# A two-block attention kernel: a hardware loop with another start and end, wq loads at other places, and a wait moved behind a branch

## The chip, the cores and the metric

The kernel runs on one core of one Trainium2 chip. The metric is the device time of one execution in microseconds (us); all times given are medians of several runs. A profile's span leaves out about 1.7 us of what is timed (777.2 against 778.9 us for the profiled run of the kernel before).

Engine names in the profile: PE is TensorE (matmul), PEld its weight loads, DVE VectorE, ACT ScalarE, POOL GpSimd, SP SyncE, which issues all loads here. A "q" behind a name (SPq) means the sequencer of that engine.

## The reference

Two independent attention blocks A and B, with the results side by side. Each has 16 batches of 64 queries, 32 heads of 128 and 512 cached keys, in bfloat16.

```python
def _A_ref(x, k_cache, v_cache, wq, wo):          # B is the same on its own data
    B, Sq, D = x.shape                            # 16, 64, 640
    H, Dh = 32, 128
    q = (x @ wq).reshape(B, Sq, H, Dh).transpose(0, 2, 1, 3)
    scores = jnp.einsum("bhqd,bhkd->bhqk", q, k_cache) * (Dh ** -0.5)
    p = softmax(scores, axis=-1)
    o = jnp.einsum("bhqk,bhkd->bhqd", p, v_cache)
    return o.transpose(0, 2, 1, 3).reshape(B, Sq, H * Dh) @ wo
return jnp.concatenate([a, b], axis=-1)
```

The caches alone are 4 x 67 MB, read once.

## The kernel before

The work is cut into 128 packs. A pack is two batches by four heads: 2 MB of K and V in four loads of 512 KB. Four packs share one x tile; 32 packs make a phase (half of the heads of one block), and each phase needs four wq and four wo blocks of 640 KB.

A plan is made in Python: each operation gets a wished time in units of packs (the table AT), each engine's program is its operations in that order, and the semaphore waits are derived. TensorE's operations are XT (transpose of x), QP (q projection), S (scores), TR (transpose of the normalised weights, two a pack), PV and OP (output projection). They are staggered, so that QP of pack n stands beside PV and OP of pack n-2.

```python
class Cfg:
    NK = 6; NV = 4; NXN = 1; NWS = 4 ...          # buffers: packs of K, of V; x tiles; wq blocks
    PERIOD = 4
    FIRST = 4
    ...
# loads: (wished time, earliest time, rank, op); SyncE issues them in this order, one after the other
for ph in range(NPH):
    for j in range(NJ):
        w = ph * NJ + j
        n0 = ph * PH + j                          # PH = 32 packs a phase
        twp = n0 + (AT["WP1"] if ph else AT["WP0"])   # when wq is copied into its place
        ...
        ready = ...                               # when the staging buffer is free again
        loads.append((twp - 0.3, ready, 1, op))
...
# TensorE's program has a period of four packs: the middle becomes a hardware loop
pe = progs["pe"]
lo = next(i for i, o in enumerate(pe) if o.kind == "QP" and o.idx == cfg.FIRST)
hi = next(i for i, o in enumerate(pe) if o.kind == "QP" and o.idx == cfg.FIRST + cfg.PERIOD)
size = hi - lo
reps = (N - 1 - cfg.FIRST) // cfg.PERIOD
...
for op in prog[:lo]:
    emit(e, op, p, {})
with e.Fori(0, reps):
    for i, op in enumerate(prog[lo:lo + size]):
        emit(e, op, p, taken)                     # ... and takes back what semaphores counted in a turn
for op in prog[lo + size * reps:]:
    emit(e, op, p, taken)
```

Softmax is computed without subtracting a maximum. A flag tells at the end whether all sums stayed in range; if not (never with these inputs), a general program runs. The end of every engine's program:

```python
def run(e, eng):
    run_program(e, eng, 0)
    if eng == "act":
        all_done(e, 0, ("d_out",))                # all stores have landed
    e.wait_ge(sems[0][("s_flc",)], 1)             # the flag is known
    with e.register("flag_" + eng) as r:
        e.reg_load(r, flag[0:1, 0:1])
        with e.If_ne(r, 128):
            all_done(e, 0)
            run_program(e, eng, 1)                # the general program, skipped by a branch
            if eng == "act":
                all_done(e, 1, ("d_out",))
```

## Time and profile before

| What | Value | Where it is read |
|---|---|---|
| time | 778.7 us | median of the runs |
| DMA rate, 20 to 738 us | 378 to 401 GB/s | the page's slices |
| TensorE's own pace | 5.4 us a pack | start to start of QP, 90 to 165 us |
| one K or V load | about 1.31 us of the DMA's time | spacing of the landings |
| one wq or wo load | about 1.7 us | the same |
| last V of the last pack lands | 755.4 us | landings |
| PV of the last pack starts | 767.1 us | timeline |
| last store issued, end of the span | 771.15, 777.2 us | timeline |

The page's slices: 40 equal stretches of the span, 19.4 us each, with PE's and the DMA's busy tenths and what the DMA moved in GB/s.

```profile
PE   3868999998978999998977999999977899999974
...
DMA  9999999999999999999999999999999999999960
GB/s 313 388 395 397 396 393 397 393 396 393 389 388 399 399 398 401 399 394 398 387 387 393 397 397 397 396 398 398 386 378 389 395 398 400 399 400 399 400 258 16
```

DMA never falls below 9 until the last two slices, while PE dips to 7 at three places. Those are the phase boundaries: up to eight weight blocks are loaded there between K and V, and TensorE waits. The page's chain that ended last, by engine, does not say so clearly:

```profile
PE 41%; SPq 25%; DMA 18%; POOL 5%; issue 5%; DVE 4%; ACT 0%; DVEq 0%; ACTq 0%
```

PE has 41% of it because the chain is followed back from the end, and late in the run PE and the DMA have nearly the same pace: a V lands 0.25 to 0.7 us before its PV.

The tail is different. PE's timeline around the loop's end (start us, busy us, engine, line, operation, tiles, shapes, count; in brackets the idle time before it and what ended it):

```profile
738.35 0.38 PE L672 MATMUL ps<-wo_sb,oT_ring 128*128 128x512 bf16 x1
740.60 0.23 PE L675 MATMUL ps<-wo_sb,oT_ring 128*128 128x128 bf16 x1 [1.87 <-issue]
...
743.38 1.09 PE L593 MATMUL ps<-kt_ring,qs_ring 32*64 32x512 bf16 x25
747.01 0.65 PE L593 MATMUL ps<-kt_ring,qs_ring 32*64 32x512 bf16 x7 [2.54 <-issue]
...
748.54 0.31 PE L675 MATMUL ps<-wo_sb,oT_ring 128*128 128x128 bf16 x1 [0.34 <-issue]
```

PE stops twice, for 1.87 and 2.54 us, and the profile shows nothing that it waited for ("issue"). The loop was left at 733.6 us, so this is straight code that runs for the first time. The trace has 16 KB packets on the queue "q8 instruction" that start at 738.0 and 744.6 us, beside each stop. After the second, matmuls take longer (0.31 us for the output projection's narrow one instead of 0.23): the granted clock is 0.5 for 3.4 us from 746.9. The same reading as sums, PE's waits from 730 to 750 us (what waited, for what: us in total, times, longest):

```profile
PE ps L593 <- issue: 2.5, 1, 2.5
PE ps L675 <- issue: 2.5, 4, 1.9
PE ps L570 <- issue: 0.3, 1, 0.3
```

Three windows of 30 to 33 us (busy us of each engine, count of instructions, granted PE clock, DMA share, GB/s); the third is a phase boundary, the other two are not:

```profile
240.00:270.00 30.00, 28.04 (x860) 20.34 (x858) 23.14 (x38) 19.57 (x54) 16.11 (x25) 1.00 1.04 399
430.00:460.00 30.00, 28.27 (x851) 20.20 (x833) 23.60 (x40) 20.93 (x57) 15.40 (x23) 1.00 1.04 397
550.00:583.00 33.00, 26.86 (x822) 19.45 (x813) 21.67 (x38) 18.89 (x52) 21.86 (x28) 1.00 1.04 379
```

SyncE's own waits are short (the rest of its time it issues: its 560 issues take 712.4 us together, one from 0.33 to 5.02 us), against 12.5 us that a load needs from issue to landing. That is the DMA's time for about nine loads of 1.31 us; in this sense the data queue is called full below, and empty, or nearly so, when the DMA's rate has fallen off at the end (59 GB/s from 750 to 760 us):

```profile
SPq L535 <- PE ps L656: 15.6, 17, 4.9
SPq L528 <- PE ps L593: 9.5, 7, 2.6
...
SPq L509 <- PE ps L549: 4.9, 3, 2.6
```

The end of ScalarE's program, from the trace's records (start us, duration in ns):

```
DMA_DIRECT2D    771.15   338    the last store
EVENT_SEMAPHORE 771.52    17    waits for the flag
TENSOR_LOAD     773.47   478    reads the flag; held back until the store has landed
COMPARE_BRANCH  773.97    54    branches over the general program
DRAIN           776.89    80    the end
```

### The profile page before, as it was taken

The numbers are of one execution on the slowest core, as the hardware profiler recorded it, in microseconds if no ns is written. First come the engines' busy times: TensorE is split into PE (matmuls) and PEld (weight loads), VectorE is DVE, ScalarE is ACT, GpSimd is POOL, SyncE is SP. The second block draws the span as 40 slices with busy tenths as digits, with TensorE's granted clock in tenths as the row PEclk, the third lists the DMA queues.
The fourth block names the chain that finished last, engine by engine and source line by source line (L and its number), as shares of the span: only waits on it lengthen the run. The fifth ranks groups of instructions, "written<-read, shape, count | busy, mean of one in ns | idle before, by whom it ended". The sixth has DMA issues, their size and how long they took to land.

```text
span 777.2 us, 44414 instructions
## 1 busy us (share of the span) xinstructions
PE 674.1 (87%) x20001; PEld 492.0 (63%) x20129; DVE 544.4 (70%) x934; ACT 484.3 (62%) x1297; POOL 404.8 (52%) x582
## 2 busy tenths in 40 slices
PE   3868999998978999998977999999977899999974
PEld 2546677676756676666654676677655567677653
DVE  3546778787767777776755777777755678787753
ACT  2546767776655667665655676777655566666642
POOL 5524455555944454544863545454575355554532
PEclk9999999999999999999999999999999999999999
DMA  9999999999999999999999999999999999999960
GB/s 313 388 395 397 396 393 397 393 396 393 389 388 399 399 398 401 399 394 398 387 387 393 397 397 397 396 398 398 386 378 389 395 398 400 399 400 399 400 258 16
DMA packets 130099, 295.24 MB, mean 380 GB/s; under 512 B 9216, under 2 KB 31744, under 8 KB 130048
## 3 DMA queue, kind: packets, MB, share of 16 engines
q1 hardware_dynamic: 127744, 292.06, 99.4%
q10 hardware_dynamic: 2304, 2.62, 0.9%
q8 instruction: 17, 0.28, 0.2%
q14 instruction: 34, 0.28, 0.1%
HBM read 292.03 MB, written 2.62 MB: 379 GB/s over the span
## 4 chain that ended last, share of the span: by engine, by line
PE 41%; SPq 25%; DMA 18%; POOL 5%; issue 5%; DVE 4%; ACT 0%; DVEq 0%; ACTq 0%
SPq L528 12%; SPq L535 11%; PE ps L570 9%; PE ps L656 9%; PE ps L593 8%; DMA v_ring<-in_B_v_cache_dram 7%; PE ps L672 6%; POOL pn_ring L628 5%; PE ps L637 5%; DMA v_ring<-in_A_v_cache_dram 5%; PE ps L675 4%; DMA wo_sb<-in_B_wo_dram 2%; DMA kn_ring<-in_B_k_cache_dram 2%; DMA wo_sb<-in_A_wo_dram 2%; DVE pT_ring L644 2%
## 5 line engine op out<-in xcount | busy, mean ns | idle before, releaser
L628 POOL TENSOR_SCALAR pn_ring<-p_ring,recip 128x512 bf16<-128x512 bf16 x512 | 344.4, 692 | 344.0 <-DVE recip L623 343.7
L608 ACT ACTIVATE p_ring<-ps 128x512 bf16<-128x512 f32 x512 | 300.6, 593 | 163.4 <-PE ps L637 160.2
L583 DVE STREAM_TRANSPOSE kt_ring<-kn_ring 128x1024 f32<-128x1024 f32 x256 | 312.8, 1229 | 79.9 <-DMA kn_ring<-in_B_k_cache_dram 47.7
L644 DVE COPY pT_ring<-ps 128x1024 bf16<-128x1024 bf16 x256 | 176.2, 688 | 78.8 <-PE ps L637 72.6
L570 PE MATMUL ps<-xT_ring,wqp_sb 128*128 128x128 bf16 x2560 | 170.6, 223 | 19.8 <-issue 13.6
L570 PEld LDWEIGHTS ps<-xT_ring,wqp_sb 128*128 128x128 bf16 x2560 | 151.0, 115 | 28.8 <-issue 16.4
L656 PE MATMUL ps<-pT_ring,v_ring 64*128 64x64 bf16 x8192 | 142.7, 191 | 24.2 <-DMA v_ring<-in_B_v_cache_dram 11.1
L593 PE MATMUL ps<-kt_ring,qs_ring 32*64 32x512 bf16 x4096 | 148.0, 398 | 8.5 <-issue 6.1
L656 PEld LDWEIGHTS ps<-pT_ring,v_ring 64*128 64x128 bf16 x8192 | 127.3, 95 | 38.9 <-DMA v_ring<-in_B_v_cache_dram 14.5
L637 PEld LDWEIGHTS ps<-ident,pn_ring 64*128 64x128 bf16 x4096 | 74.6, 95 | 108.6 <-ACT oT_ring L663 58.9
L663 ACT ACTIVATE oT_ring<-ps 128x512 bf16<-128x512 f32 x128 | 76.4, 597 | 95.0 <-PE ps L656 73.5
L675 PE MATMUL ps<-wo_sb,oT_ring 128*128 128x128 bf16 x512 | 112.8, 220 | 23.2 <-issue 18.1
L637 PE MATMUL ps<-ident,pn_ring 64*128 64x64 bf16 x4096 | 105.1, 192 | 17.2 <-DVE pT_ring L644 11.2
L672 PE MATMUL ps<-wo_sb,oT_ring 128*128 128x512 bf16 x384 | 119.4, 382 | 0.0
L608 ACT ACTIVATION_READ_ACCUMULATOR p_ring<-ps 128x1 f32 x512 | 101.7, 199 | 0.0
L576 ACT ACTIVATE qs_ring<-ps 128x512 bf16<-128x512 f32 x128 | 76.4, 597 | 23.4 <-PE ps L570 23.4
L672 PEld LDWEIGHTS ps<-wo_sb,oT_ring 128*128 128x128 bf16 x512 | 50.1, 98 | 53.3 <-issue 1.1
L593 PEld LDWEIGHTS ps<-kt_ring,qs_ring 32*64 32x64 bf16 x4096 | 56.0, 104 | 42.7 <-issue 8.0
L685 DVE TENSOR_TENSOR acc<-acc,ps 128x128 f32<-128x128 f32 x96 | 27.4, 285 | 37.4 <-PE ps L675 37.2
L675 PEld LDWEIGHTS ps<-wo_sb,oT_ring 128*128 128x128 bf16 x512 | 50.5, 99 | 2.2 <-issue 2.2
L623 DVE RECIPROCAL recip<-rowsum 128x2 f32<-128x2 f32 x256 | 35.5, 139 | 2.6 <-ACT p_ring L608 2.6
L542 POOL COPY wqp_sb<-ws_ring 128x1280 bf16<-128x1280 bf16 x16 | 20.0, 1253 | 15.6 <-DMA ws_ring<-in_A_wq_dram 8.2
(24 smaller groups left out, 115.6 us busy)
## 6 DMA issues: line engine op xcount, KB each, us to landing
kn_ring<-in_A_k_cache_dram SPq DMA_DIRECT2D x128, 512.0 KB, 12.5
v_ring<-in_A_v_cache_dram SPq DMA_DIRECT2D x128, 512.0 KB, 12.3
kn_ring<-in_B_k_cache_dram SPq DMA_DIRECT2D x128, 512.0 KB, 12.5
v_ring<-in_B_v_cache_dram SPq DMA_DIRECT2D x128, 512.0 KB, 10.8
ws_ring<-in_A_wq_dram SPq DMA_DIRECT2D x8, 640.0 KB, 12.7
wo_sb<-in_A_wo_dram SPq DMA_DIRECT2D x8, 640.0 KB, 12.6
ws_ring<-in_B_wq_dram SPq DMA_DIRECT2D x8, 640.0 KB, 12.3
wo_sb<-in_B_wo_dram SPq DMA_DIRECT2D x8, 640.0 KB, 12.3
```

What stands on the lines that cost most here:

```text
L528: ins = e.dma_start(kn_ring[:, n % NK, b, :], src)
L535: ins = e.dma_start(v_ring[:, n % NV, b].rearrange("p a t d -> p a (t d)"), src)
L570: last = e.matmul(ps[:, 0, f * 128:(f + 1) * 128], w[:, kt, f, :], xT_ring[:, xs, kt, :], start=(kt == 0), stop=(kt == KT - 1))
L583: ins = e.transpose(dst, kn_ring[:, n % NK, b, :].bitcast(F32))
L593: last = e.matmul(ps[64 * b:64 * b + 64, i, :], qs_ring[rows, n % NQ, f, b, :], kt_ring[rows, n % NKT, b, :, f // 2, :, f % 2], start=(f = ...
L608: ins = e.activation(dst, src, ACTF.Exp, scale=1.0, accum_out=rowsum[:, h:h + 1])
L628: ins = e.tensor_scalar(pn_ring[:, (h // 2) % NPN, :, h % 2, :], p_ring[:, (h // 2) % NP, :, h % 2, :], recip[:, (h // 2) % NR, h % 2:h % ...
L637: last = e.transpose(pt_flat[:, b, 64 * t:64 * t + 64], pn_ring[rows, op.idx % NPN, t].rearrange("q s k -> q (s k)"), ident[rows, rows], t ...
L644: ins = e.tensor_copy(pT_ring[:, op.idx % NT].rearrange("p b t q -> p b (t q)"), pt_flat)
L656: last = e.matmul(o_ps[:, s, col:col + 64], v_ring[rows, n % NV, b, a, t, :], pT_ring[rows, (2 * n + a) % NT, b, t, :], start=(t == 0), st ...
L672: last = e.matmul(out_ps0, oT, wo_sb[:, 4 * j + h4, 0:N0], start=(j == 0 and h4 == 0), stop=(j == NJ - 1 and h4 == 3))
L675: last = e.matmul(out_ps1, oT, wo_sb[:, 4 * j + h4, N0:D], start=(h4 == 0), stop=(h4 == 3))
```

## The change

The intent: straight code costs TensorE instruction fetches, so nearly all packs should lie in the loop. (In the trace before, eight of the 17 packets of 16 KB on the instruction queue start from 23.0 to 69.2 us and nine from 738.0 us on, none in between, while the loop of about 1,280 TensorE records repeats. The head's stops at 31.9, 37.5, 43.3 and 49.2 us lie 255 or 256 TensorE records apart, with one packet for each; so much code is called a page below.) If the loop begins at a TR right behind an OP (instead of at a QP), it can run one turn longer, and the head and the tail are shorter. For this the program needs one more XT at its end, whose result nobody reads, because each turn holds one. The wq loads of the next phase are not left to the phase boundary. The wait for the last store moves behind the flag's branch.

```diff
-    FIRST = 4
+    FIRST = 5
...
-    for g in range(N // NJ):
+    for g in range(N // NJ + 1):
         n0 = g * NJ
         txt = n0 + AT["XT"]
         add("pe", "XT", g, txt, [("xn", g % cfg.NXN), ("ident",)], [("OUTB",)])
+        if g == N // NJ:
+            break
...
-            loads.append((twp - 0.3, ready, 1, op))
+            loads.append((twp - 0.3 if not ph else ready + 2.0 + 0.15 * PH, ready, 1, op))
...
-    lo = next(i for i, o in enumerate(pe) if o.kind == "QP" and o.idx == cfg.FIRST)
-    hi = next(i for i, o in enumerate(pe) if o.kind == "QP" and o.idx == cfg.FIRST + cfg.PERIOD)
+    lo = next(i for i, o in enumerate(pe) if o.kind == "TR" and o.idx == cfg.FIRST)
+    hi = next(i for i, o in enumerate(pe) if o.kind == "TR" and o.idx == cfg.FIRST + 2 * cfg.PERIOD)
     size = hi - lo
-    reps = (N - 1 - cfg.FIRST) // cfg.PERIOD
+    last_qp = max(o.idx for o in pe[lo:hi] if o.kind == "QP")
+    reps = 1 + (N - 1 - last_qp) // cfg.PERIOD
...
             run_program(e, eng, 0)
-            if eng == "act":
-                all_done(e, 0, ("d_out",))
             e.wait_ge(sems[0][("s_flc",)], 1)
...
                     if eng == "act":
                         all_done(e, 1, ("d_out",))
+            if eng == "act":
+                all_done(e, 0, ("d_out",))
```

What it does to the programs: the loop has 31 turns instead of 30 and the same 25 operations in another rotation. Behind it stand TR, PV, TR, OP, TR, PV, OP and the flag's matmul instead of 31 operations. The wq loads of phases 2, 3 and 4 are issued at packs 6 to 9, 39 to 42 and 71 to 74 instead of 18 to 34, 60 to 66 and 95 to 98. DVE's, ACT's and POOL's operations stay as they were.

## The prediction

> **What bounds the kernel now.** The DMA engines. The page's slices show DMA at 9 and 386 to 401 GB/s from 20 us to about 745 us. The trace's landings give a K or V half (512 KB) about 1.31 us each, a wq or wo block (640 KB) about 1.7 us, whatever TensorE does. [...]this trace never passes 402. TensorE needs about 5.4 us a pack when nothing is missing (start to start of the q projections, 90 to 165 us), in all 691 us against the DMA's 750. In the last phase V lands 0.3 to 0.7 us before its use.
>
> The last V lands at 755.4 us, the span ends at 777.2. In the timeline TensorE leaves the hardware loop at 733.6 us and stands for 1.87 us (738.7) and 2.54 us (744.5) ("issue"); 16 KB packets on the instruction queue start at 738.0 and 744.6. After the second the granted clock is halved for 3.4 us. The packs that begin there take 7.3 and 9.8 us instead of 5.4: 6.3 us late, and V(123) to V(127) lie waiting 3 to 12 us. [...] At the end the last store is issued at 771.15, its landing is waited for until 773.5, then ScalarE reads the flag (0.48), branches, and drains only at 776.9.
>
> **What changes.**
> 1. Loop: 31 turns instead of 30, beginning 1.5 packs earlier and leaving 1.5 packs before the end instead of 4. Head stalls (31.9 to 65.5 us, about 10 us) shrink by a third, worth nothing: the DMA queue runs full under them. Tail: the two stalls and the half clock go, -6.3 us. The exit moves to about 753 us, when the data queue is nearly empty[...]. One extra transpose of x: +0.4.
> 2. wq loads: those of phases 2 to 4 move from packs 18 to 34, 60 to 66 and 95 to 98 to just after the previous phase boundary (packs 6 to 9, 39 to 42, 71 to 74). Same bytes, same DMA time. TensorE's starvation (packs 56 to 68, 93 to 100) is halved at the boundary and reappears a few packs later. The bytes that must land before pack 101 are the same, so the last phase starts at the same time: about 0.
> 3. The store's wait after the branch: flag read and branch overlap the store: -1.9 us.
> The last V no longer waits for a late PV: -0.5.
>
> Sum: 778.7 - 6.3 + 0.7 + 0.4 - 1.9 - 0.5 = 771.1 us. Range 766.5 to 775.5. Faster by over 2%: 0.06; within 2%: 0.92; slower: 0.02.
>
> **What would show it right.** V of the last pack lands at 752 to 756 us; DMA slices stay 385 to 401 GB/s; no "issue" gap over 1 us between 700 and 750; PV of the last pack 6 us after the last V landing instead of 11.7; end 4 us after the last store's issue instead of 6.
>
> **What would make it wrong.** If the DMA has slack hidden behind its busy share, spreading wq moves the last V landing forward by several us. If leaving the loop costs a cold fetch of 3 us or a halved clock, half the gain is lost.

The sum came to 771.1 us. The sum's +0.7 us stands for the estimate for the code fetched at the loop's new exit, given without a measured fetch. The other terms stand: -6.3 us for the two packs in which TensorE stops (7.3 and 9.8 us instead of 5.4), +0.4 for a transpose of x (its five matmuls take 0.44 us in the trace before), -1.9 for the wait for the store (771.52 to 773.47 us), and -0.5 for the last V, an estimate too. 402 GB/s is the highest of the trace's windows of 10 us.

## The result

The changed kernel takes 769.99 us (769.60 to 770.28, 4 runs) against 778.75 us (777.88 to 779.17, 4 runs). The ratio is 0.9889, with a 95% interval of 0.9871 to 0.9906. It is 8.7 us less and inside the predicted range, 1.1 us below the predicted sum. (Ratios here and below are the mean time of one kernel's fast runs over that of the other's of the same rounds, so not quite the ratio of the medians quoted.)

The slices after, each 19.2 us:

```profile
PE   3868999999987799999996779999998799999995
...
DMA  8999999999999999999999999999999999999991
GB/s 312 388 385 386 398 397 398 396 397 398 397 385 388 388 398 400 399 399 399 397 393 391 383 391 397 396 387 398 398 398 391 391 399 398 400 399 399 400 396 60
```

The DMA stays at its rate, and again PE dips, now at other places. PE's last slice is 5 and not 4: a smaller part of the tail is idle. The chain by engine:

```profile
SPq 55%; DMA 21%; PE 18%; issue 3%; DVE 1%; POOL 0%; ACT 0%; DVEq 0%
```

The chain is now more than half SyncE's issuing (from 20 us on, one issue lasts 0.33 to 4.87 us). The kernel has not become DMA-bound by the change. It was so before, but PE now follows within 0.3 us of each V from pack 84 to 125, and so the chain has to go through the loads.

PE's timeline where it leaves the loop (the branch is at 753.28 us; lines of the file are 3 higher than before):

```profile
752.51 0.41 PE L640 MATMUL ps<-ident,pn_ring 64*128 64x64 bf16 x16
753.07 0.22 PE L678 MATMUL ps<-wo_sb,oT_ring 128*128 128x128 bf16 x1 [0.16 <-issue]
...
753.67 0.38 PE L675 MATMUL ps<-wo_sb,oT_ring 128*128 128x512 bf16 x1
753.89 0.22 PE L678 MATMUL ps<-wo_sb,oT_ring 128*128 128x128 bf16 x1
754.04 0.41 PE L640 MATMUL ps<-ident,pn_ring 64*128 64x64 bf16 x16
755.33 1.11 PE L659 MATMUL ps<-pT_ring,v_ring 64*128 64x64 bf16 x64 [0.88 <-DVE pT_ring L647]
```

There is no stop: TR, OP and TR run on, and PV then waits 0.88 us for DVE, which is the ordinary dependence. PE's waits from 730 to 750 us have one line left, with a longest of 0.2 us (a missing record rather than a wait: of the four wide matmuls of each output projection, 512 in all, this trace and that of the kernel before have 384):

```profile
PE ps L678 <- issue: 0.6, 4, 0.2
```

The landing of a pack's last V and the start of its PV, in us, from the traces:

| Pack | before: V lands | PV starts | after: V lands | PV starts |
|---|---|---|---|---|
| 122 | 734.5 | 735.1 | 734.3 | 734.4 |
| 123 | 739.7 | 742.3 | 739.6 | 739.7 |
| 124 | 745.0 | 752.2 | 744.9 | 745.2 |
| 125 | 750.2 | 757.5 | 750.1 | 750.4 |
| 126 | 752.7 | 762.4 | 752.7 | 755.3 |
| 127 | 755.4 | 767.1 | 756.7 | 760.0 |

At pack 122 the two kernels are 0.7 us apart. (In between, the changed one is up to 7.4 us later, from pack 40 to 92, because its wq blocks lie ahead of K and V there; at pack 96 they are level again.) So the first 735 us, with all the moved loads, gave next to nothing. The last five packs gave 7.1 us. From the last store's issue to the end it is 3.9 us (764.08 to 768.0) instead of 6.0 (771.15 to 777.2), 2.1 us.

The same three windows after:

```profile
240.00:270.00 30.00, 22.22 (x679) 15.74 (x675) 17.01 (x30) 15.38 (x41) 12.60 (x19) 1.00 1.05 389
430.00:460.00 30.00, 21.95 (x665) 15.57 (x655) 17.72 (x31) 15.60 (x43) 11.89 (x18) 1.00 1.05 388
550.00:583.00 33.00, 31.66 (x989) 23.28 (x987) 26.07 (x45) 22.57 (x61) 25.12 (x34) 1.00 1.04 397
```

The starvation has moved as foreseen: at 240 and 430 us PE is busy 22 us instead of 28, at 550 us it is busy 31.7 instead of 26.9. SyncE now waits 20.5 us for the x tile's one buffer (it did 4.9 us), since the plan puts x loads earlier, and much less for V's buffers (L538, before L535):

```profile
SPq L512 <- PE ps L552: 20.5, 5, 5.1
...
SPq L538 <- PE ps L659: 1.9, 6, 0.6
```

These waits, of at most 5.1 us, are shorter than the 12.5 us of loads already queued, and the DMA's rate (383 to 400 GB/s in the slices from 19 to 749 us) does not show them.

### The profile page after: what moved, and what is told of

Its sections match the earlier page's. It is cut to its first block, busy times and chain, and to the rows that moved or that the text cites. A ratio compares the mean times of both kernels' runs of the same rounds, so it can differ in the third digit from the quotient of the medians.

```text
span 768.0 us, 44433 instructions
## 1 busy us (share of the span) xinstructions
PE 675.2 (88%) x20006; PEld 491.6 (64%) x20134; DVE 545.6 (71%) x934; ACT 483.8 (63%) x1297; POOL 405.9 (53%) x582
## 4 chain that ended last, share of the span: by engine, by line
SPq 55%; DMA 21%; PE 18%; issue 3%; DVE 1%; POOL 0%; ACT 0%; DVEq 0%
SPq L538 26%; SPq L531 25%; DMA v_ring<-in_A_v_cache_dram 11%; DMA v_ring<-in_B_v_cache_dram 6%; PE ps L659 5%; PE ps L573 4%; PE ps L596 3%; PE ps L675 2%; PE ps L640 2%; SPq L512 2%; DMA wo_sb<-in_B_wo_dram 2%; DMA kn_ring<-in_B_k_cache_dram 2%; DMA wo_sb<-in_A_wo_dram 1%; PE ps L678 1%; SPq L518 1%
## 5 line engine op out<-in xcount | busy, mean ns | idle before, releaser
L640 PE MATMUL ps<-ident,pn_ring 64*128 64x64 bf16 x4096 | 105.1, 192 | 26.9 <-DVE pT_ring L647 20.0
## 6 DMA issues: line engine op xcount, KB each, us to landing
kn_ring<-in_A_k_cache_dram SPq DMA_DIRECT2D x128, 512.0 KB, 12.5
```

Of the source, the lines that this page charges most:

```text
L640: last = e.transpose(pt_flat[:, b, 64 * t:64 * t + 64], pn_ring[rows, op.idx % NPN, t].rearrange("q s k -> q (s k)"), ident[rows, rows], t ...
```

## The experiments

The theory: until the last loads are issued the DMA sets the time, and so moved wq loads and shorter head stops are worth nothing. The gain is the tail's two stops with the clock halved after them, and the overlap at the end. Rivals: (a) the gain is spread over the run, from wq loads no longer bunched; (b) from fewer stops at the head; (c) TensorE, at 5.4 us a pack, is what limits, and the rotation of the loop makes it faster.

The first four ran on one chip, beside 11 runs of the kernel before (778.4 us); the last four on another, beside 11 more (778.53 us).

### The parts alone

The edits are those of the change's diff: loop_only has the two hunks around `FIRST`, `lo`, `hi`, `reps` and the extra XT; wq_only the one line of `loads.append`; exit_only the moved `all_done`; no_wq all but the wq line. In short:

```diff
 # loop_only, beside the extra XT
-    lo = next(... if o.kind == "QP" and o.idx == cfg.FIRST)                 # FIRST = 4
+    lo = next(... if o.kind == "TR" and o.idx == cfg.FIRST)                 # FIRST = 5
 # wq_only
-            loads.append((twp - 0.3, ready, 1, op))
+            loads.append((twp - 0.3 if not ph else ready + 2.0 + 0.15 * PH, ready, 1, op))
 # exit_only: behind the branch instead of ahead of the flag's wait
+            if eng == "act":
+                all_done(e, 0, ("d_out",))
 # no_wq, from the changed kernel
-            loads.append((twp - 0.3 if not ph else ready + 2.0 + 0.15 * PH, ready, 1, op))
+            loads.append((twp - 0.3, ready, 1, op))
```

> The loop part of the change alone (31 turns, from transpose to output projection, with the extra transpose of x); wq loads and the final waits as before. Theory (DMA-bound until the last loads, gain made in the tail): about 6.5 us less than before, near 772 us; the last V lands within 2 us of where it did before (755.4), but the last PV starts 6 to 7 us sooner; no issue gap over 1 us after 700 us. Rival (the gain is spread over the run, from shorter head stalls or from wq): less than 3 us of gain here, or the last V landing moves by as much as the time.

> The wq part alone. Theory: the bytes ahead of pack 101 are the same and the DMA queue is never empty, so within 1 us of before, near 778.7 us, with TensorE's starvation moved to packs 39 to 42 and 71 to 74. Rival (bursts of weights at the phase boundary cost time): 3 us or more faster than before.

> The moved wait for the last store alone. Theory: ScalarE's flag read and branch overlap the store, 1.9 to 2.1 us less than before, near 776.7 us; the end comes 3.9 to 4 us after the last store is issued instead of 6. Rival (the branch is bound by something that ends as late as before): no change.

> The changed kernel with wq loads ordered as before, so loop and final wait together. Theory: as the changed kernel, 769 to 771 us. Rival (spreading wq has a share in the gain): 773 us or more.

| Kernel | us (median, range, runs) | ratio to before, 95% interval | us of difference from the ratio |
|---|---|---|---|
| loop_only | 772.87 (771.99 to 774.84, 6) | 0.9932 (0.9916 to 0.9947) | -5.3 |
| wq_only | 778.20 (777.50 to 780.51, 6) | 0.9999 (0.9986 to 1.0012) | -0.1 |
| exit_only | 775.39 (775.23 to 775.76, 6) | 0.9963 (0.9951 to 0.9976) | -2.9 |
| no_wq | 769.93 (769.76 to 770.53, 5) | 0.9893 (0.9879 to 0.9906) | -8.3 |

The last column is (1 - ratio) times 778.4. The parts add up: 5.3 + 2.9 = 8.2 against 8.3 for both. The wq loads give nothing, alone or with the others: rival (a) falls. In wq_only the two stops stand as before (PE's waits from 700 us on):

```profile
PE ps L593 <- issue: 2.5, 1, 2.5
PE ps L675 <- issue: 1.9, 1, 1.9
```

In loop_only no stop is left after 700 us:

```profile
PE ps L659 <- DVE pT_ring L647: 1.7, 2, 0.9
PE ps L640 <- ACT oT_ring L666: 0.7, 1, 0.7
PE ps L675 <- ACT oT_ring L666: 0.7, 1, 0.7
```

The last PV starts at 761.6 us, 5.4 us sooner than before and not the expected 6 to 7. That run had the clock halved once more in the tail, from 758.0 us: its last pack took 5.85 us instead of the 4.67 of the changed kernel, which is 1.2 us and most of the gap to 760.0. Its six runs spread over 2.9 us, those of the changed kernel over 0.7.

exit_only gave more than expected. In its profile the last store is issued at 769.70 and the span ends at 773.50: 3.8 us instead of 6.05, so 2.25 us come from where they were expected. The rest lies before the store: 0.7 us by the ratio, 1.45 us in this pair of profiles. In the profiled run, the second stop was shorter, 1.1 us and not 2.5:

```profile
PE ps L675 <- issue: 1.9, 1, 1.9
...
PE ps L593 <- issue: 1.1, 1, 1.1
```

There the clock was halved from 740.9 us, between the two stops. So PE came later to the place of the second stop, beside which the packet starts as before (744.5 and 744.6 us), and went on at the same time (746.94 and 747.01 us), but then at the full clock, where the kernel before has 3.4 us of half clock. That accounts for the 1.45 us of this pair. But the edit does not touch TensorE's program, and why six runs out of six came out low is not settled: no_wq, too, is 3.0 us below loop_only (8.3 less 5.3), more than the 2 us expected of this edit. It may be where the halved clock falls; no run tells.

### The head and the exit, one turn each

late_start has `FIRST = 13`: the loop begins one turn later, and is left at the same place. early_exit has one turn less: it begins as in the change, and is left 22 us sooner.

```diff
-    FIRST = 5
+    FIRST = 13                                             # late_start
...
-    reps = 1 + (N - 1 - last_qp) // cfg.PERIOD
+    reps = (N - 1 - last_qp) // cfg.PERIOD                 # early_exit
```

> The changed kernel with the loop beginning one turn later (30 turns), the exit where it was: four more packs of straight code at the head, so more stalls there. Theory (head stalls run under a full DMA queue): two to four more issue gaps of 1 us or more before 110 us, but the time of the changed kernel, 769 to 771 us. Rival (the earlier start has a share in the gain): at least 2 us slower than the changed kernel.

> The changed kernel with one turn fewer (30), so the loop is left about 22 us sooner, while the DMA queue is full, and five and a half packs of straight code follow. Theory (a page of code fetched behind a full queue stops TensorE about 2 us, one fetched from an idle queue nearly nothing): one or two issue gaps of about 2 us between 735 and 750 us, often a halved clock after them; 774 to 778 us, 4 to 8 us slower than the changed kernel. Rival (the gain came from the boundary's place in the pack, transpose instead of projection): within 1 us of the changed kernel.

late_start: 769.85 us (769.61 to 770.14, 4 runs), ratio 0.9888 (0.9874 to 0.9903). early_exit: 775.67 us (774.96 to 777.45, 6 runs), ratio 0.9971 (0.9957 to 0.9985).

PE's "issue" waits from 20 to 110 us in late_start:

```profile
PE ps L596 <- issue: 5.9, 2, 3.6
PE ps L640 <- issue: 4.7, 2, 2.5
PE ps L573 <- issue: 3.3, 2, 1.7
PE ps L659 <- issue: 2.9, 3, 1.4
```

and in the changed kernel:

```profile
PE ps L596 <- issue: 2.4, 1, 2.4
PE ps L640 <- issue: 2.2, 1, 2.2
...
PE ps L573 <- issue: 1.5, 1, 1.5
PE ps L659 <- issue: 1.4, 2, 1.2
```

The four lines add up to 16.8 us against 7.5, with eight stops over 1 us against four, and the time is the same: its ratio to the kernel before is 0.9888, that of the changed kernel 0.9889. Stops of TensorE at the head are free, as long as the loads behind it go on: rival (b) falls.

early_exit's timeline where it leaves the loop:

```profile
737.60 0.38 PE L675 MATMUL ps<-wo_sb,oT_ring 128*128 128x512 bf16 x1
738.60 0.23 PE L678 MATMUL ps<-wo_sb,oT_ring 128*128 128x128 bf16 x1 [0.62 <-issue]
...
741.37 1.10 PE L596 MATMUL ps<-kt_ring,qs_ring 32*64 32x512 bf16 x25
744.73 0.57 PE L596 MATMUL ps<-kt_ring,qs_ring 32*64 32x512 bf16 x7 [2.25 <-issue]
...
746.18 0.31 PE L678 MATMUL ps<-wo_sb,oT_ring 128*128 128x128 bf16 x1 [0.34 <-issue]
```

The stops are back, 0.62 and 2.25 us, with the clock halved from 744.9 us for 3.4 us. PV of packs 123 and 124 follow their predecessors after 6.0 and 9.65 us, and the time is 5.8 us above late_start's on the same chip, most of the gain. This kernel has the change's rotation of the loop and its wq loads; it differs in when the loop is left, and so also in having 33 operations behind the loop instead of 8. The trace has instruction packets at 736.2 and 742.4 us, while the data queue was full; the further ones (748.7, 752.4 and on) came as it emptied, and no "issue" stop over 0.34 us stands beside them. In the changed kernel the first is at 756.4 us, when the DMA's rate has fallen from 394 GB/s (740 to 745 us) to 10 (756 to 758 us), and none costs a stop. The two kernels leave the loop at the same place of the same code: the first packet starts 4.4 us after the branch here, and 3.1 us after it in the changed kernel. So what counts is when the straight code runs, and not only how much of it there is: behind a full data queue a page cost 0.6 to 2.5 us in these tails, behind an empty one nothing that shows. How the queue delays the fetch, these runs do not show.

### Fewer bytes

Wrong results on purpose: only the first four wq blocks are loaded; the copies into place still run, on old data.

```diff
-            op = add("sp", "LDWQ", w, twp - 0.5, [], [("ws", w % cfg.NWS)])
             ready = -99.0
+            if w < cfg.NWS:
+                op = add("sp", "LDWQ", w, twp - 0.5, [], [("ws", w % cfg.NWS)])
...
-            loads.append((twp - 0.3 if not ph else ready + 2.0 + 0.15 * PH, ready, 1, op))
+            if w < cfg.NWS:
+                loads.append((twp - 0.3, ready, 1, op))
```

> Wrong results on purpose: the changed kernel without the twelve wq loads after the first four (the copies of wq still run, on old data), 7.9 MB less. Theory (DMA-bound): 12 x 1.7 us = about 20 us less than the changed kernel, 749 to 754 us, the last V landing sooner by the same. Rival (TensorE sets the pace, as its 5.4 us a pack lie close to the DMA's): less than 8 us.

749.85 us (749.52 to 750.36, 4 runs), ratio 0.9633. That is 20.1 us less than the changed kernel (20.0 less than late_start, on the same chip), 1.7 us for each of the twelve loads left out. The slices, 18.7 us each:

```profile
PE   3869999999998998999988999989998899899995
...
GB/s 316 386 395 396 398 397 397 397 397 397 397 384 400 397 401 400 399 399 398 398 390 393 396 398 396 398 397 398 398 398 382 395 400 400 399 400 399 399 348 32
```

The rate is nearly as before (396 GB/s from 20 to 720 us, against 395) and the bytes are fewer, so the time falls with the bytes: rival (c) falls as an account of the kernel's time.

It is right in two things. The rotation does make TensorE faster: in the kernel before, QP stands for 0.39 us ("issue") behind the loop's branch once a turn, 11.2 us in all from 75 to 730 us, and in loop_only, behind the same branch at its new place, no such wait is left. Where V lies ready (packs 8 to 23), PV follows PV every 5.40 us before and every 5.29 us in fewer_bytes. But TensorE then only waits longer for V: by pack 122 the changed kernel is 0.7 us ahead, and early_exit, which has the rotation too, loses 5.8 us. And TensorE is close behind the DMA. Here PE is at 9 in most slices, and at the end the last V landed 7.3 us before its PV (732.5 and 739.8 us). It landed 24.2 us sooner than in the changed kernel and not the expected 20; the last PV came 20.1 us sooner, so 4 us of it were lost to TensorE's tail. With still fewer bytes, TensorE would probably soon be the limit (an estimate, from these 7.3 us and from its 5.29 us a pack).

### A faster version

Since each engine's branch over the general program takes 2.7 to 3.7 us in the changed kernel (2.66 us on ScalarE, 3.25 on VectorE, 3.29 on SyncE and 3.55 on GpSimd from the branch to the next record; TensorE's own branch record lasts 3.66), the end should come sooner if an engine branches while it would be idle anyway. In late_ops, VectorE's last two sums and the last store (given to SyncE) stand behind the branch, once in the general case, once in the other.

```diff
+        late = (dve0[-2:], act0[-1:])             # left out of run_program
+        def run_late(e, eng):
+            for op in late[0] if eng == "dve" else late[1] if eng == "sp" else []:
+                emit(e, op, 0, {})
...
                 with e.If_ne(r, 128):
+                    run_late(e, eng)
                     all_done(e, 0)
...
+                with e.If_eq(r, 128):
+                    run_late(e, eng)
-            if eng == "act":
+            if eng == "sp":
                 all_done(e, 0, ("d_out",))
```

> An attempt at a faster version: the changed kernel, with the last two sums of VectorE and the last store (now SyncE's) placed after each engine's branch on the flag, so that these branches run while TensorE still works. Theory: the end comes 3 us after the last store is issued instead of 3.9, if VectorE's branch (about 3.2 us, begun at the flag, 760.4) does not delay its sums by more than 0.6 us: 0.3 to 1 us faster than the changed kernel. Rival: the delay eats it, no change or slower.

769.23 us (768.97 to 769.46, 4 runs), ratio 0.9880; late_start, as fast as the changed kernel, had 769.85 us (769.61 to 770.14) in the same rounds. The ranges do not meet, so it is about 0.6 us faster, the best of all, though by less than one thousandth. The store is issued at 764.90 and the span ends at 767.55, 2.65 us later instead of 3.9. But VectorE's branch (3.6 us from 760.25) held up its sums: they start at 763.99 us, 4.3 us after the last PV (759.7), while in the changed kernel it is 3.2 us (763.16 and 760.0). That gave back 1.2 us.

## Why the prediction was right

- **What bounds it: right.** fewer_bytes shows it: 7.9 MB less, 20.1 us less. (The lowest slice of the page before is 378 GB/s, not 386 as the prediction says, and V's 0.3 to 0.7 us before its use hold for packs 112 to 122, not for the whole last phase.)
- **Tail, -6.3 us for the stops and the half clock, +0.7 for the exit, +0.4 for the transpose, -0.5 for the last V: net -5.7; loop_only measured -5.3.** The stops are gone in the changed kernel and return in early_exit. The exit's +0.7, the author's estimate, was too much: no stop shows there. The transpose costs 0.28 us on PE in the chain. That the net fits so well is partly luck: the +0.7 and the -0.5 were both wrong and nearly cancel. The -0.5 was wrong: the last V did not land sooner but 1.3 us later (756.7 against 755.4). In the traces it lands at 756.3 to 757.5 us in the kernels that issue the last store but one at 748.6 to 749.9 us (changed, loop_only, no_wq, late_start, late_ops) and at 755.1 to 755.9 us in those that issue it at 754 us or later (before, wq_only, exit_only, early_exit). The store may get in its way; this was not tested. It cost nothing, because PE came 3.3 us after it.
- **wq loads, about 0: right.** wq_only measured a ratio of 0.9999. The starvation moved to the packs named.
- **Head stops worth nothing: right.** late_start has 9.3 us more of them and takes the same time.
- **The wait behind the branch, -1.9 us: too small.** The runs give -2.9 (exit_only), of which its profile shows 2.25 at the end itself. 0.7 us are open.
- **Signs in the profile.** Last V between 752 and 756 us: missed by 0.7 us. DMA at 385 to 401 GB/s: 383 in one slice. No stop over 1 us from 700 to 750: right. Last PV 6 us after its V: it was 3.3 us. End 4 us after the last store's issue: 3.9 us.
- **The sum, 771.1 us:** measured 769.99. The loop's net term was about right, and most of the 1.1 us left is the term of the branch, put at 1.9 us and measured at 2.9.

## What to carry to other kernels

Before costing a stall, ask which resource it holds up: 9 us more of stopped TensorE at the head cost nothing here, and 2.9 to 4.4 us at the end, with a slower clock behind them, cost 5 to 6, because too few loads were left after them for the DMA to stay the slower one. (In an exit as late as this one little straight code is left, too.) If a loop has to be left, leave it when the data queue is empty, or nearly so: left 22 us sooner, behind a full queue, this kernel took 5.8 us more. And rearranging loads without removing bytes gained nothing where the DMA queue was never empty (wq_only: 778.20 us against 778.4); it only moved the place where the engines starve.
